# Attention and a gated feed-forward layer: the end of a query softmax moved back in VectorE's queue, four buffers for decode and sums, 64-wide kv, queries in place

## The chip, the cores and the metric

One core of a Trainium2 chip runs the whole program. The metric is the device time of one execution in microseconds; the figure before is the median of three runs. Names: PE is TensorE (PEld its weight loads), DVE is VectorE, ACT is ScalarE, POOL is GpSimd, SP the engine that issues most DMAs.

## The reference

All data are float32. There are 8 sequences of 576 tokens, 8 heads of 64. The attention has no matrix of scores: queries are softmaxed over the 64 numbers of a head, keys over the sequence, and a 64x64 matrix kv per sequence and head stands between them. Its output, 4608 tokens of 512 numbers, goes through a layer of 2048 hidden units.

```python
q_s = exp(q - max(q, axis=-1)); q_s = q_s / (sum(q_s, axis=-1) + 1e-09)
k_s = exp(k - max(k, axis=2));  k_s = k_s / (sum(k_s, axis=2) + 1e-09)
kv  = einsum('bhsd,bhse->bhde', k_s, v)
x   = einsum('bhsd,bhde->bhse', q_s, kv)      # then (4608, 512)
h   = x @ w_in                                 # 512 x 2048
g   = h * clip(h + 3, 0, 6) / 6
out = g @ w_out                                # 2048 x 512
```

## The kernel before

**Numbers.** Weights come as 64-bit patterns. `decode(f)` turns the pattern of hidden chunk f (128 hidden units, f from 0 to 15) into float32 in the tile v (tag v, a ring of three buffers of 4 KB a partition) and `split`s it into a high part (a cast on ACT) and a low part (a subtraction on DVE), so that a product is three matmuls: high by high, high by low, low by high. `decode` costs ACT three instructions (the absolute value into m, the scaling of raw, the cast to w) and DVE five (two on m, two on v, the subtraction to w).

**Stages.** Tokens 0 to 1535 are three blocks j = 0, 1, 2 of 512. For each block and each chunk f, `gemm1` makes ph = x times w_in (12 matmuls), `relu6` makes g (one instruction on ACT, one on DVE), `split_ahead` makes its two parts gp, and `gemm2` adds 12 matmuls to four accumulators po (four PSUM banks for the whole block, one for each 128 tokens). `store` takes po out of PSUM at the block's end, alternately on ACT and DVE, and writes it out. The remaining 3072 tokens are three superblocks of 1024 (`phase1`, `phase2`), which use a scheme of seven products instead of eight; the sums of weight blocks that it needs are made by `sum_weights` during blocks 1 and 2.

**The attention of the next stage runs between the chunks.** Four head pairs hp of two heads each. `attention(j, hp)` serves blocks 0 and 1, `token_attention` the rest. Each is a generator whose pieces are called by `steps` between the chunks: keys (maximum, exponential, transposes pe and pe2, copies to ke), queries (maximum qm, exponentials with their sums qr, division, transposes tp, copy to qT), then `kv_of` (products pkv, rk, kv) and the product px of kv with qT, whose result is split into the next block's x. In `attention` for block 1 the query softmax is eight ACT instructions of 64 columns with the sum taken along; DVE then adds EPS to qr, takes the reciprocal and multiplies.

**kv.** For two heads, kv is a 128x128 tile with the two 64x64 matrices on the diagonal and zeros elsewhere, made by one DVE instruction that multiplies by a mask; px of both heads is then one matmul. A float32 matmul is two instructions in the profile. Only superblocks 1 and 2 have kv for their new sequences as 128x64 tiles (`narrow`), and run px in 64x64 quarters of PE, each head in a PSUM bank of its own.

**The order of the work.** A scheduler orders each engine's instructions by a cost model and by priorities; `ahead` notes the last instruction of g, gp and w on each engine in `front`, and `behind` makes its work issue after those. From block 1 on PE keeps the order in which the program is written (`in_order`); the other engines, and PE in block 0, stand in the order that the scheduler chose. Each engine and SP's queue then run strictly in that order.

**sum_weights.** Each pair of chunks and each side takes two v buffers: w4 (the weights, loaded from DRAM for pairs 3 to 7) and sums (four combinations). Both are split in place and stored by four DMAs (`keep`). Pairs from DRAM take two calls, and one call is made per chunk, from chunk 4 of block 1 on.

Of the kernel before, what the change touches and what calls it, by code (L numbers as in the profile page):

```python
# [19 lines left out]
P = 128  # L20
# [13 lines left out]
def attention_moe(  # L34
# [63 lines left out]
    mask = const.tile([P, P], F32, name="mask")  # L98
    nc.gpsimd.memset(mask, 0.0)
    nc.gpsimd.memset(mask[0:D, 0:D], 1.0)  # L100
    nc.gpsimd.memset(mask[D:P, D:P], 1.0)
# [44 lines left out]
    def decode(f):  # L146

        n = 2 * DM
        pairs = raws.pop(f).rearrange("p (n two) -> p n two", two=2)
        low, high = pairs[:, :, 0], pairs[:, :, 1]  # L150
        m = moe.tile([P, n], F32, name="m", bufs=1)
        nc.scalar.activation(m, high.bitcast(F32), AF.Abs)
        nc.vector.tensor_scalar(m, m, W_MIN, W_MAX, op0=ALU.max, op1=ALU.min)
        m = m.bitcast(U32)
        nc.vector.tensor_scalar(
            m, m, 3, 0x3FFFFFFF, op0=ALU.logical_shift_left, op1=ALU.bitwise_and
        )
        v = moe.tile([P, n], F32, name="v", bufs=3)
        vu = v.bitcast(U32)
        nc.vector.scalar_tensor_tensor(  # L160
            vu, high, 0xC0000000, m, op0=ALU.bitwise_and, op1=ALU.bitwise_or
        )
        nc.scalar.activation(low, low, AF.Copy, scale=2.0**-29)
        nc.vector.tensor_tensor(vu, vu, low, op=ALU.add)
# [19 lines left out]
    narrow = set()  # L184
# [8 lines left out]
    first = {}  # L193

# [12 lines left out]
    def kv_of(hp, batches, quarters=False):  # L207
        n = len(batches)
        both = bank_a("pkv")[:, 0 : n * (D + 1)].rearrange("p (b d) -> p b d", b=n)
        for i, (_, ke, vt) in enumerate(batches):  # L210
            for c in range(NCH):
                for h in range(2):
                    hs = slice(h * D, (h + 1) * D)
                    mm(both[hs, i], ke[:, c, hs], vt[:, c, h, :], c == 0, c == NCH - 1, n > 1)
        rk = att.tile([P, 2], F32, name="rk", bufs=2)[:, 0:n]
        nc.vector.tensor_scalar_add(rk, both[:, :, D], EPS)
        nc.vector.reciprocal(rk, rk)
        for i, (b, _, _) in enumerate(batches):
            kv = att.tile([P, P], F32, name="kv", bufs=10)
            if quarters:  # L220
                nc.vector.tensor_scalar_mul(kv[:, 0:D], both[:, i, 0:D], rk[:, i : i + 1])
                kvs[b, hp] = kv
                narrow.add((b, hp))
                continue
            nc.vector.scalar_tensor_tensor(
                kv.rearrange("p (h d) -> p h d", h=2),
                both[:, i : i + 1, 0:D].broadcast_to([P, 2, D]),
                rk[:, i : i + 1],
                mask.rearrange("p (h d) -> p h d", h=2),
                op0=ALU.mult,  # L230
                op1=ALU.mult,
            )
            kvs[b, hp] = kv
# [6 lines left out]
    def q_softmax(qt, lean, pool):  # L240
# [18 lines left out]
        nc.vector.tensor_scalar_add(qr, qr, EPS)  # L259
# [16 lines left out]
    def attention(j, hp):  # L276
# [3 lines left out]
        else:  # L280
# [9 lines left out]
        q_softmax(qt, j > 0, nc.vector if j else nc.gpsimd)  # L290
# [5 lines left out]
        if j:  # L296
            qT = att.tile([P, TB], F32, name="qT")
# [54 lines left out]

    held = {}
# [7 lines left out]
    def token_attention(t0, n, hp, put):  # L361
# [40 lines left out]
        kv_of(hp, list(zip(new, ke, vt)), t0 >= START + SB)  # L402
# [8 lines left out]
    def sb_attention(s):  # L411
        def put(t0, hp, need, qT):

            if not s:
                for c in range(SB // TB):
                    px = bank_a("px")
                    for b, lo, hi in segments(need, t0 + c * TB):
                        mm(px[:, lo:hi], kvs[b, hp], qT[:, c * TB + lo : c * TB + hi], True, True)
# [4 lines left out]
            for both in zip_longest(*(segments(need, t0 + c * TB) for c in range(2))):  # L423
                for c, part in enumerate(both):
                    if part:
                        b, lo, hi = part
                        for h, r in enumerate(rows):
                            mm(
                                px[h][rows[c], lo:hi],
                                kvs[b, hp][r, slice(0, D) if (b, hp) in narrow else r],  # L430
# [11 lines left out]
    def block_attention(j):  # L442
        def put(t0, hp, need, qT):
            px = bank_a("px")
            for b, lo, hi in segments(need, t0):
                mm(px[:, lo:hi], kvs[b, hp], qT[:, lo:hi], True, True)
# [35 lines left out]
    def sum_weights(pair, side):  # L482

        w4 = moe.tile([P, 2 * DM], F32, name="v", bufs=3)
# [10 lines left out]
        sums = moe.tile([P, 2 * DM], F32, name="v", bufs=3)  # L495
# [86 lines left out]
    def phase1(s):  # L582
        xb, yb, zb = {}, {}, {}
        for i, (p, n) in enumerate(SLOTS1):
# [24 lines left out]
            with tc.high_priority():  # L609
# [14 lines left out]
                if n == 6:  # L624
                    nc.vector.tensor_add(h21, h21, y)
                    r = moe.tile([P, 2 * DM], F32, name="v", bufs=3)
# [3 lines left out]
    def phase2(s):  # L630
# [30 lines left out]
        def outs(name):  # L661
            return moe.tile([P, 2 * DM], F32, name="v", bufs=3).rearrange("p (c n) -> p c n", c=2)
# [107 lines left out]
    def store(j, po):  # L770
        for t in range(NTT):
            if j == NB - 1:
                ob = moe.tile([P, 2 * DM], F32, name="v", bufs=3)[:, 0:DM]
# [67 lines left out]
    for j in range(NB):  # L841
        if j == 1:
            in_order.append(True)
        if j < NB - 1:
# [4 lines left out]
            else:  # L849
                step = steps(units, 3, (2,))  # L850
# [3 lines left out]
        for n, f in enumerate(chunks):  # L854
# [9 lines left out]
            if j > 1 or j and n > 3:  # L864
# [99 lines left out]
```

## Time and profile before

| | |
|---|---|
| runs | 827.92, 828.76, 829.11 us; median 828.76 |
| profiled execution | 827.1 us; span 825.3 us, mean granted clock 0.996 |
| busy | PE 97%, DVE 82%, ACT 55%, POOL 7% of the span |
| PE idle, 0 to 35.83 us | 13.4 us (loads, block 0's own attention, first decodes) |
| PE idle, 35.83 to 140.73 us (block 0) | 4.3 us |
| PE idle, 140.73 to 337.11 us (blocks 1, 2) | 3.8 us |
| PE idle, 337.11 us to the end (superblocks) | 4.9 us |

The span is the time from the first to the last instruction; 1.8 us lie around it. A row of the timeline has the start, the duration, the engine, the line, the operation, the tile written and those read, and in brackets the idle time before it with what ended it. Matmul ends are modelled, and back-to-back matmuls overlap, so their pace is taken from long groups.

### The profile page before, as it was taken

The page shows a single profiled execution, that of the slowest core. Times are in us where ns is not written, and L with a number is a line of the kernel's source. Part 1 is how long each engine was busy: PE and PEld are TensorE (multiplying, and loading weights), DVE is VectorE, ACT ScalarE, POOL GpSimd, SP SyncE. Part 2 cuts the span into 40 slices and gives each one's busy share as a digit, 9 for nine tenths or more (in the row PEclk, how much of TensorE's full clock was granted, in tenths as well). Part 3 has the DMA queues.
Part 4 walks back from the last instruction along what each step waited for, and adds up shares of the span by engine and source line. Part 5 has one row for each costly group of instructions (what it writes and reads, how often), then busy time and mean ns, then how long its engine had stood idle before and what let it go on. Part 6 is the DMA issues. An engine that isn't in the chain of part 4 may idle for free.

```text
span 825.3 us, 11783 instructions
## 1 busy us (share of the span) xinstructions
PE 798.8 (97%) x4088; PEld 641.3 (78%) x4088; DVE 673.4 (82%) x1064; ACT 454.1 (55%) x733; POOL 55.7 (7%) x155
## 2 busy tenths in 40 slices
PE   4899899999989999999999999999999999999998
PEld 3577678888877778887877788777788888888886
DVE  7998998589979888888999994798699836658873
ACT  7897673334444445556556653565556535445543
POOL 5000001010111110001003000011000000000000
PEclk9999999999999999999999999999999999999999
DMA  9999676245579873888786677775566776666673
GB/s 368 416 407 334 199 263 225 59 163 189 192 239 341 288 263 128 267 279 277 272 279 213 187 233 251 226 234 183 178 184 199 238 247 197 187 201 185 197 218 114
DMA packets 75803, 192.30 MB, mean 233 GB/s; under 512 B 7264, under 2 KB 19808, under 8 KB 73696
## 3 DMA queue, kind: packets, MB, share of 16 engines
q1 hardware_dynamic: 75024, 190.38, 70.1%
q10 hardware_dynamic: 720, 1.18, 0.4%
q8 instruction: 32, 0.52, 0.3%
q14 instruction: 27, 0.22, 0.1%
HBM read 147.49 MB, written 44.04 MB: 232 GB/s over the span
## 4 chain that ended last, share of the span: by engine, by line
PE 69%; DVE 16%; DMA 7%; ACT 4%; issue 3%; SPq 1%; POOL 1%; DVEq 0%; ACTq 0%; POOLq 0%
PE x L88 29%; PE z L88 11%; PE y L88 11%; PE ph L88 7%; PE po L88 7%; DMA wf<-v 4%; DMA qt<-in_qf_dram 2%; PE px L88 2%; DVE g L580 1%; PE pkv L88 1%; DVE v L160 1%; DVE qt L343 1%; DVE v L121 1%; DVE gp L121 1%; DVE m L350 1%
## 5 line engine op out<-in xcount | busy, mean ns | idle before, releaser
L121 ACT CAST gf<-g 128x512 fp32r<-128x512 f32 x168 | 104.2, 622 | 97.5 <-DVE gf L121 37.0
L88 PE MATMUL po<-w,gp 128*128 128x512 f32 x576 | 145.5, 399 | 3.6 <-DVE gp L779 2.1
L88 PE MATMUL ph<-x,w 128*128 128x512 f32 x576 | 142.7, 394 | 3.2 <-ACT w L121 2.0
L121 DVE TENSOR_TENSOR gf<-g,gf 128x512 fp32r<-128x512 f32 x168 | 112.9, 686 | 25.3 <-ACT gf L121 24.9
L88 PEld LDWEIGHTS ph<-x,w 128*128 128x128 f32 x576 | 107.8, 188 | 29.6 <-ACT w L121 3.0
L88 PEld LDWEIGHTS po<-w,gp 128*128 128x128 f32 x576 | 106.7, 189 | 29.2 <-DVE gp L779 2.5
L88 PE MATMUL x<-right,gp 128*128 128x512 f32 x384 | 94.6, 391 | 0.4 <-ACT g L616 0.4
L88 PE MATMUL x<-gf,gp 128*128 128x512 f32 x384 | 94.1, 390 | 0.0
L88 PEld LDWEIGHTS x<-gf,gp 128*128 128x128 f32 x384 | 71.9, 188 | 15.7 <-DVE gf L121 0.4
L88 PEld LDWEIGHTS x<-right,gp 128*128 128x128 f32 x384 | 71.6, 188 | 15.7 <-ACT g L616 0.8
L579 ACT ACTIVATE g<-ph,three 128x512 f32<-128x512 f32 x48 | 32.7, 684 | 38.1 <-PE ph L88 38.1
L88 PE MATMUL y<-right,gp 128*128 128x512 f32 x192 | 49.1, 391 | 0.0
L88 PE MATMUL x<-right,left 128*128 128x512 f32 x192 | 47.7, 392 | 0.0
L88 PE MATMUL x<-gf,left 128*128 128x512 f32 x192 | 47.0, 390 | 0.0
L88 PE MATMUL z<-gf,gp 128*128 128x512 f32 x192 | 46.9, 390 | 0.0
L333 POOL COPY swap<-qm 32x32 f32<-32x32 f32 (+1 forms) x64 | 19.6, 306 | 355.3 <-DVE qm L341 353.3
L121 ACT CAST gp<-g 128x512 fp32r<-128x512 f32 x48 | 29.7, 619 | 23.8 <-DVE g L580 23.7
L88 PEld LDWEIGHTS z<-gf,gp 128*128 128x128 f32 x192 | 36.0, 188 | 7.8 <-DVE gf L121 0.4
L88 PEld LDWEIGHTS x<-gf,left 128*128 128x128 f32 x192 | 35.9, 188 | 7.7 <-ACT v L702 0.2
L88 PEld LDWEIGHTS y<-right,gp 128*128 128x128 f32 x192 | 35.8, 188 | 7.6 <-issue 0.2
L88 PEld LDWEIGHTS x<-right,left 128*128 128x128 f32 x192 | 35.7, 188 | 7.6
L580 DVE SCALAR_TENSOR_TENSOR g<-g,ph 128x512 f32<-128x512 f32 x48 | 32.6, 680 | 9.2 <-ACT g L579 9.1
(139 smaller groups left out, 1279.8 us busy)
## 6 DMA issues: line engine op xcount, KB each, us to landing
gp<-wf SPq DMA_DIRECT2D x112, 512.0 KB, 4.2
left<-wf SPq DMA_DIRECT2D x56, 512.0 KB, 4.2
raw<-in_w_dram SPq DMA_DIRECT2D x16, 1024.0 KB, 13.6
wf<-v SPq DMA_DIRECT2D x64, 256.0 KB, 3.2
wf<-w SPq DMA_DIRECT2D x48, 256.0 KB, 4.5
vt<-in_v_dram SPq DMA_DIRECT2D x28, 325.0 KB, 5.6
kt<-in_kT_dram SPq DMA_DIRECT2D x28, 288.0 KB, 3.8
ke<-in_k_dram SPq DMA_DIRECT2D x24, 320.0 KB, 5.1
```

The lines of the kernel that those rows point to most:

```text
L88: nc.tensor.matmul(out, lhsT, rhs, start=start, stop=stop, skip_group_check=goes_on)
L121: return nc.scalar.copy(hi, src), nc.vector.tensor_sub(lo, src, hi.bitcast(F32))
L160: nc.vector.scalar_tensor_tensor(vu, high, 0xC0000000, m, op0=ALU.bitwise_and, op1=ALU.bitwise_or)
L333: nc.gpsimd.tensor_copy(swap[r : r + QD], stat[o : o + QD])
L343: nc.vector.tensor_sub(qs, qs, across(qm))
L350: nc.vector.transpose(qT, qt)
L579: ahead(nc.scalar.activation(r, h, AF.Relu, bias=three, scale=1.0))
L580: ahead(nc.vector.scalar_tensor_tensor(g, r, 6.0, h, op0=ALU.min, op1=ALU.mult))
```

## The change

1. In block 1's attention the query softmax stops after the exponentials (`yield`); the addition of EPS to qr comes a step later and is made to issue after the instructions in `front`, so on DVE behind the last g, gp or w of the next chunk. Each unit has four steps instead of three, and its last piece (px) is called in the second step of the next unit.
2. Queries are softmaxed, transposed and stored back in one tile of two halves, used in turn by the head pairs; the tiles qt and qT of before are gone, so that pair hp+1 can be loaded while pair hp is still in use.
3. kv is always 128x64; the mask is gone; every px is two 64x64 matmuls (`heads`), here with both heads in one PSUM bank.
4. The ring of v has four buffers, and the sums begin one chunk earlier.

```diff
-        v = moe.tile([P, n], F32, name="v", bufs=3)
+        v = moe.tile([P, n], F32, name="v", bufs=4)
...
-            kv = att.tile([P, P], F32, name="kv", bufs=10)
-            if quarters:
-                nc.vector.tensor_scalar_mul(kv[:, 0:D], both[:, i, 0:D], rk[:, i : i + 1])
...
-            nc.vector.scalar_tensor_tensor(
-                kv.rearrange("p (h d) -> p h d", h=2),
-                both[:, i : i + 1, 0:D].broadcast_to([P, 2, D]),
-                rk[:, i : i + 1],
-                mask.rearrange("p (h d) -> p h d", h=2),
...
+            kv = att.tile([P, D], F32, name="kv", bufs=10)
+            nc.vector.tensor_scalar_mul(kv, both[:, i, 0:D], rk[:, i : i + 1])
             kvs[b, hp] = kv
...
-        nc.vector.tensor_scalar_add(qr, qr, EPS)
+        with ExitStack() as order:
+            if lean:
+                yield
+
+                for ins in front.values():
+                    order.enter_context(tc.issue_after(ins.ins))
+            nc.vector.tensor_scalar_add(qr, qr, EPS)
         nc.vector.reciprocal(qr, qr)
...
-            qt = att.tile([P, TB], F32, name="qt", bufs=1)
-            nc.sync.dma_start(qt, q[j, hp])
-            qt = qt.rearrange("p (c h d) -> p c h d", c=NC4, h=2)
+            if "q" not in held:
+                held["q"] = att.tile([P, SB], F32, name="qt", bufs=1)
+            qT = held["q"][:, hp % 2 * TB : (hp % 2 + 1) * TB]
+            nc.sync.dma_start(qT, q[j, hp])
+            qt = cut(qT, 0, NC4, 2, D)
...
-        q_softmax(qt, j > 0, nc.vector if j else nc.gpsimd)
+        yield from q_softmax(qt, j > 0, nc.vector if j else nc.gpsimd)
...
-        if j:
-            qT = att.tile([P, TB], F32, name="qT")
         nc.scalar.copy(qT, tp)
...
-                mm(px[:, lo:hi], kvs[b, hp], qT[:, lo:hi], True, True)
+                heads(px, lo, hi, kvs[b, hp], qT, True)
...
+    def heads(px, lo, hi, kv, qT, start):
+
+        for h in range(2):
+            r = slice(h * D, (h + 1) * D)
+            mm(px[r, lo:hi], kv[r], qT[r, lo:hi], start, True, True)
...
-                step = steps(units, 3, (2,))
+                step = steps(units, 4, (1,))
...
-            if j > 1 or j and n > 3:
+            if j > 1 or j and n > 2:
                 behind(sums)
```

What it does to the order, at three places. First ACT in block 0, around 40 us, before (g_356 is the first chunk's g and gp_359 its high part, m and raw belong to decode, kt and ke to the keys of head pair 0 of block 1, qt and qr to its queries):

```order
L152 ACTIVATE m_467<-raw_4_122 128x1024
L265 ACTIVATE kt_373<-kt_373,km_380 128x576
L121 CAST gp_359<-g_356 128x512
L121 CAST w_3_426<-v_422 128x2x512
L272 COPY ke_375<-pe_429 128x512
L273 COPY ke_375<-pe2_430 64x128
L121 CAST gp_415<-g_412 128x512
L163 ACTIVATE raw_7_397<-raw_7_397 128x1024
L247 ACTIVATE qt_378,qr_384<-qt_378,qm_383 128x64 x8
L579 ACTIVATE g_461<-ph_448,three_84 128x512
```

The same place after:

```order
L148 ACTIVATE m_450<-raw_4_118 128x1024
L574 ACTIVATE g_356<-ph_343,three_80 128x512
L256 ACTIVATE kt_373<-kt_373,km_380 128x576
L574 ACTIVATE g_409<-ph_396,three_80 128x512
L117 CAST w_3_423<-v_419 128x2x512
L232 ACTIVATE qt_378,qr_384<-qt_378,qm_383 128x64 x6
L117 CAST gp_359<-g_356 128x512
L232 ACTIVATE qt_378,qr_384<-qt_378,qm_383 128x64 x2
L117 CAST gp_412<-g_409 128x512
L263 COPY ke_375<-pe_461 128x512
```

The two g and six of the eight exponentials now stand ahead of the cast of the first chunk's g, and so does the cast of w_3.

Second DVE in block 0, where the query softmax of head pair 1 ends, before (qm is the maximum, qr the sums):

```order
L121 TENSOR_TENSOR w_8_761<-v_756,w_8_761 128x2x512
L580 SCALAR_TENSOR_TENSOR g_808<-g_808,ph_795 128x512
L245 TENSOR_REDUCE qm_552<-qt_547 128x8
L121 TENSOR_TENSOR gp_811<-g_808,gp_811 128x512
L259 TENSOR_SCALAR qr_553<-qr_553 128x8
L260 RECIPROCAL qr_553<-qr_553 128x8
L261 TENSOR_TENSOR qt_547<-qt_547,qr_553 128x512
```

After; its maximum (qm_550) stands 28 places further up:

```order
L117 TENSOR_TENSOR w_6_603<-v_598,w_6_603 128x2x512
L250 TENSOR_SCALAR qr_551<-qr_551 128x8
L156 SCALAR_TENSOR_TENSOR v_654<-raw_7_394,m_650 128x1024
L117 TENSOR_TENSOR x1_611<-px_606,x1_611 128x512
L117 TENSOR_TENSOR gp_591<-g_588,gp_591 128x512
L251 RECIPROCAL qr_551<-qr_551 128x8
```

The addition to the sum stood two places behind the maximum and now stands 28 behind it.

Third DVE at the end of block 1, before (v_2091 is a sum, gp_2354 and gp_2359 the evictions of po, g_2292 the g of block 2's first chunk):

```order
L580 SCALAR_TENSOR_TENSOR g_2292<-g_2292,ph_2279 128x512
L497 TENSOR_TENSOR v_2091<-v_2022 128x256
L499 TENSOR_TENSOR v_2091<-v_2022 128x256
L350 STREAM_TRANSPOSE m_2340<-qt_2302 128x1024
L368 TENSOR_REDUCE km_2471<-kt_2461 128x1
L498 TENSOR_TENSOR v_2091<-v_2091,v_2022 128x256
L396 TENSOR_TENSOR ke_2255<-ke_2255,pm_2313 128x640
L396 TENSOR_TENSOR ke_2259<-ke_2259,pm_2313 128x640
L121 TENSOR_TENSOR gp_2295<-g_2292,gp_2295 128x512
L779 TENSOR_SCALAR gp_2354<-po_1365 128x512
```

After (the g is g_2303, the sum v_2309):

```order
L331 TENSOR_TENSOR qm_2346<-qm_2346,swap_2349 128x32
L340 TENSOR_TENSOR qt_2324<-qt_2324,qm_2346 128x1024
L342 TENSOR_REDUCE qr_2347<-qt_2324 128x32
L575 SCALAR_TENSOR_TENSOR g_2303<-g_2303,ph_2290 128x512
L363 TENSOR_REDUCE km_2497<-kt_2487 128x1
L391 TENSOR_TENSOR ke_2266<-ke_2266,pm_2339 128x640
L391 TENSOR_TENSOR ke_2270<-ke_2270,pm_2339 128x640
L331 SCALAR_TENSOR_TENSOR qr_2347<-qr_2347,swap_2358 128x32
L117 TENSOR_TENSOR gp_2306<-g_2303,gp_2306 128x512
L492 TENSOR_TENSOR v_2309<-v_2234 128x256
L494 TENSOR_TENSOR v_2309<-v_2234 128x256
L774 TENSOR_SCALAR gp_2380<-po_1366 128x512
```

The sum moved from directly behind g to directly ahead of the first eviction, and the softmax of the next unit (qt, qr) from ahead of g by a whole unit to just ahead of it.

From block 1 on, PE's order differs only in the px products.

More of the change, by code (lines that the diff above doesn't have):

```diff
@@ L97, in attention_moe @@
     make_identity(nc, ident)
[L98 to L101, printed above, removed]
     three = const.tile([P, 1], F32, name="three")
@@ L183, in attention_moe @@
     kvs = {}
-    narrow = set()
     def cut(t, at, *shape):
@@ L193, in attention_moe @@
     first = {}
+    held = {}
     def load_first(hp):
@@ L205, in load_first_v, with kv_of @@
         nc.sync.dma_start(first[hp][3], v[0, hp])
-    def kv_of(hp, batches, quarters=False):
+    def kv_of(hp, batches):
         n = len(batches)
@@ L218, in kv_of @@
         for i, (b, _, _) in enumerate(batches):
-            kv = att.tile([P, P], F32, name="kv", bufs=10)
-            if quarters:
[L221 to L225, printed above, removed]
-                kv.rearrange("p (h d) -> p h d", h=2),
-                both[:, i : i + 1, 0:D].broadcast_to([P, 2, D]),
-                rk[:, i : i + 1],
-                mask.rearrange("p (h d) -> p h d", h=2),
-                op0=ALU.mult,
-                op1=ALU.mult,
-            )
+            kv = att.tile([P, D], F32, name="kv", bufs=10)
+            nc.vector.tensor_scalar_mul(kv, both[:, i, 0:D], rk[:, i : i + 1])
             kvs[b, hp] = kv
@@ L351, in q_softmax_t @@
         return qT
-    held = {}
     def x_of(s):
@@ L401, in token_attention @@
         yield
-        kv_of(hp, list(zip(new, ke, vt)), t0 >= START + SB)
+        kv_of(hp, list(zip(new, ke, vt)))
         yield
@@ L417, in put @@
                     for b, lo, hi in segments(need, t0 + c * TB):
-                        mm(px[:, lo:hi], kvs[b, hp], qT[:, c * TB + lo : c * TB + hi], True, True)
+                        heads(px, lo, hi, kvs[b, hp], qT[:, c * TB : (c + 1) * TB], True)
                     nc.scalar.copy(x_of(s)[:, hp, c * TB : (c + 1) * TB], px)
@@ L429, in put @@
                                 px[h][rows[c], lo:hi],
-                                kvs[b, hp][r, slice(0, D) if (b, hp) in narrow else r],
+                                kvs[b, hp][r],
                                 qT[r, c * TB + lo : c * TB + hi],
@@ L445, in put @@
             for b, lo, hi in segments(need, t0):
-                mm(px[:, lo:hi], kvs[b, hp], qT[:, lo:hi], True, True)
+                heads(px, lo, hi, kvs[b, hp], qT, True)
             x_hi, x_lo = x_block(j)
@@ L482, in sum_weights @@
     def sum_weights(pair, side):
-        w4 = moe.tile([P, 2 * DM], F32, name="v", bufs=3)
+        w4 = moe.tile([P, 2 * DM], F32, name="v", bufs=4)
         if pair < FROM_DRAM:
@@ L494, in sum_weights @@
         a11, a12, a21, a22 = (q1, q3, q2, q4) if side else (q1, q2, q3, q4)
-        sums = moe.tile([P, 2 * DM], F32, name="v", bufs=3)
+        sums = moe.tile([P, 2 * DM], F32, name="v", bufs=4)
         s1, s3, s2, s4 = (sums[:, n * HT : (n + 1) * HT] for n in range(4))
@@ L625, in phase1 @@
                     nc.vector.tensor_add(h21, h21, y)
-                    r = moe.tile([P, 2 * DM], F32, name="v", bufs=3)
+                    r = moe.tile([P, 2 * DM], F32, name="v", bufs=4)
                     relu6(gb, r, gb)
@@ L661, in outs @@
         def outs(name):
-            return moe.tile([P, 2 * DM], F32, name="v", bufs=3).rearrange("p (c n) -> p c n", c=2)
+            return moe.tile([P, 2 * DM], F32, name="v", bufs=4).rearrange("p (c n) -> p c n", c=2)
         def send(t, r, c):
@@ L772, in store @@
             if j == NB - 1:
-                ob = moe.tile([P, 2 * DM], F32, name="v", bufs=3)[:, 0:DM]
+                ob = moe.tile([P, 2 * DM], F32, name="v", bufs=4)[:, 0:DM]
             else:
```

## Prediction

> **What bounds the kernel now.** I read the page first, then the busy time by stage, then the waits, and last the timeline at each place where TensorE (PE) waits.
>
> ```profile
> span 825.3 us, 11783 instructions
> PE 798.8 (97%) x4088; PEld 641.3 (78%) x4088; DVE 673.4 (82%) x1064; ACT 454.1 (55%) x733; POOL 55.7 (7%) x155
> ```
>
> PE is busy 97% of the span, so what can be won is its idle time and what can be lost is any work added to it. The stretches below are: up to the first full use of w_2, the rest of block 0, block 1, block 2, the superblocks.
>
> ```profile
> core 0: us, PE busy (x) PEld busy (x) DVE busy (x) ACT busy (x) POOL busy (x), PEclk, DMA share, GB/s
> 0.00:35.83 35.83, 22.40 (x150) 16.48 (x151) 30.30 (x54) 28.44 (x41) 12.85 (x25) 0.95 0.97 388
> 35.83:140.73 104.90, 100.61 (x503) 78.17 (x504) 98.74 (x144) 77.22 (x155) 2.43 (x10) 0.98 0.82 292
> 140.73:245.85 105.12, 103.00 (x554) 83.01 (x553) 85.99 (x167) 43.84 (x69) 11.71 (x40) 1.00 0.52 169
> 245.85:337.11 91.26, 89.61 (x492) 72.41 (x493) 79.83 (x140) 42.94 (x66) 9.79 (x32) 1.00 0.74 255
> 337.11:825.28 488.17, 483.23 (x2390) 391.27 (x2390) 378.52 (x562) 261.69 (x405) 18.90 (x48) 1.00 0.70 219
> ```
>
> PE idles 4.3 us in the rest of block 0, 2.1 in block 1, 1.7 in block 2. The superblocks keep their PE order and idle 4.9 of 488 us; the change has nothing to win or lose there. In block 0 VectorE (DVE) is nearly as full as PE (98.7 of 104.9 us). The waits of that stretch:
>
> ```profile
> DVE qr L259 <- ACT qt L247: 2.6, 2, 2.0
> PE ph L88 <- ACT w L121: 2.0, 1, 2.0
> PE ph L88 <- DVE w L121: 1.1, 3, 0.5
> PE tp L94 <- DVE qt L261: 0.9, 2, 0.6
> ```
>
> DVE waits 2.0 us for the exponentials of head pair 1, decode runs late behind it, and PE then waits 2.0 us for w_10. That wait costs more than itself:
>
> ```profile
> 91.14:94.56 3.42, 1.54 (x8) 1.09 (x9) 3.42 (x6) 3.18 (x6) 0.00 (x0) 1.00 0.55 211
> 94.56:97.97 3.41, 3.41 (x9) 2.63 (x9) 3.41 (x5) 2.75 (x15) 0.00 (x0) 0.50 0.69 217
> 97.97:101.38 3.41, 3.41 (x18) 2.76 (x17) 3.31 (x7) 3.20 (x7) 0.00 (x0) 1.00 0.67 254
> ```
>
> After a stretch of 3.4 us in which PE was busy for 1.54, the granted clock is 0.50 for 3.41 us: 9 matmuls, not 18, so 1.7 us lost. Block 0 thus holds 4.3 + 1.7 = 6.0 us that could be won.
>
> **The change, part by part.**
>
> *The end of the softmax behind g, queries in place.* The DVE wait above goes: the sum of head pair 1 now stands far behind its maximum. With two halves in the query ring, pair 1's query loads and is exponentiated while pair 0's is still in use, so 16 exponentials fall into the stretch from 40 to 52 us instead of 8, and the DVE g of chunk 0 stands three instructions later. That hits ScalarE (ACT) where it is full:
>
> ```profile
> 35.45 1.25 ACT L579 ACTIVATE g<-ph,three 128x512 f32<-128x512 f32 x2
> 36.95 1.14 ACT L152 ACTIVATE m<-raw 128x1024 f32<-128x1024 f32 x1 [0.25 <-DVE v L160]
> 37.99 0.76 ACT L265 ACTIVATE kt<-kt,km 128x576 f32<-128x576 f32 x1
> 38.65 0.61 ACT L121 CAST gp<-g 128x512 fp32r<-128x512 f32 x1
> 39.70 1.05 ACT L121 CAST w<-v 128x1024 fp32r<-128x1024 f32 x1 [0.44 <-DVE v L164]
> ...
> 42.97 2.66 ACT qt L247 x16
> ```
>
> Before, the cast of chunk 0's g ends at 38.65 + 0.61 = 39.26. After, it stands behind m (1.04 from start to start), two g (0.62 each), the key's exponential (0.66), the cast of w_3 (0.96) and six of the eight exponentials (6/8 of 2.66 = 2.0; the 16 rows are eight exponentials with their reads). The m still waits for the decode step that ended at 36.95: 36.95 + 5.9 + 0.61 = 43.5, so 4.2 us later. PE's next instruction is the second product of chunk 0, which reads this cast:
>
> ```profile
> 38.81 0.76 PE L94 MATMUL pe<-ident,kt 128*128 128x128 f32 x5 [0.39 <-ACT kt L265]
> 39.33 2.08 PE L88 MATMUL po<-w,gp 128*128 128x512 f32 x8
> ```
>
> PE, whose order here is unchanged, therefore stands still from about 39.6 to 43.5, longer than the pause that halved the clock above, so I add 1.7: 5.9 us. What it would have waited until w_4 (0.6 for tp, the longest of its row of waits, and 0.3 in the row of DVE's w) is then covered, 0.9 less: 5.0 us late. Bounds: 0, if nothing is held up, and 5.9. I take 5.0, since each instruction ahead of the cast is in the built order.
>
> From there PE is about 5 us behind a decode that is itself 3 us late (six of pair 1's exponentials stand ahead of the cast of w_4 too: 2.0 us, and about 1 us of DVE's own waits). That leaves some 2 us of slack or more, so the later waits of block 0 go: 4.3 of idle time, less the 0.9 above and the 0.39 at pe, is 3.0, most of it the 2.0 for w_10; with the clock's 1.7, 4.7 us are won back (between 3.0 and 4.7).
>
> *64-wide kv.* DVE gets a shorter eviction:
>
> ```profile
> L225 DVE SCALAR_TENSOR_TENSOR kv<-pkv,rk,mask 128x128 f32<-128x128 f32 x20 | 6.5, 339 | 0.0
> L221 DVE TENSOR_SCALAR kv<-pkv,rk 128x64 f32<-128x64 f32 x12 | 3.0, 277 | 0.1
> ```
>
> 62 ns each, four of them ahead of w_2: 0.25 us won. On PE each px becomes two 64x64 products on the diagonal quarters. The superblocks already run 64x64 quarters, and show what entering and leaving them costs:
>
> ```profile
> 589.22 2.20 PE L88 MATMUL x<-gf,gp 128*128 128x512 f32 x9
> 591.35 1.09 PE L88 MATMUL px<-m,kv 64*64 64x448 f32 x12
> 592.37 1.65 PE L88 MATMUL y<-right,left 128*128 128x512 f32 x6
> ...
> 159.15 1.76 PE L88 MATMUL ph<-x,w 128*128 128x512 f32 x7
> 160.74 1.03 PE L88 MATMUL px<-m,kv 128*128 128x128 f32 x4
> 161.61 0.27 PE L94 MATMUL pm<-ident,km 128*128 128x128 f32 x1
> 161.64 2.09 PE L88 MATMUL po<-w,gp 128*128 128x512 f32 x8
> ...
> 149.04 2.72 PE po L88 x12
> ```
>
> From the end of x (591.42) to the end of y (594.02) are 2.60 us; six matmuls at 2.72/12 = 0.227 take 1.36, leaving 1.24 for px in quarters. From the end of ph (160.91) to the end of po (163.73) are 2.82; less 1.81 for eight matmuls and 0.11 for pm, 0.90 for a whole px of the same 512 columns. A px in quarters costs 0.34 more. Blocks 1 and 2 of the loop hold eight such groups (four units of block 2, four of the first superblock): 2.7 us, and nothing hides it, since PE is the bound there. In block 0 there are six (pairs 2 and 3 have theirs in two pieces): 2.0 us. The four of block 0's own attention stand in PE's idle start. Bounds: 0, if two quarters cost no switch, and 0.34 each.
>
> That needs the two heads to run side by side. In the px row above the quarters' four streams of 512 columns take together what one whole px takes, and there each bank takes both column halves at once; never two row halves, since each head has its own bank. Now both heads write one bank, in different partitions. By the nearest row I take it as free. The Trainium skill (TensorEngine Tiling, "Gotcha 1: PSUM Pressure") says: "Different row tiles cannot access same PSUM bank simultaneously"; no run here shows it, and by that rule each px would take its columns twice, which is rival B.
>
> *Four buffers of v, sums a chunk earlier.* In blocks 1 and 2, DVE waits with a sum for the stores that still read its buffer, and what stands behind it is the eviction of po:
>
> ```profile
> 236.62 0.68 DVE L580 SCALAR_TENSOR_TENSOR g<-g,ph 128x512 f32<-128x512 f32 x1
> 240.25 0.43 DVE L497 TENSOR_TENSOR v<-v 128x256 f32<-128x256 f32 x1 [2.95 <-DMA wf<-v]
> 245.12 0.68 DVE L779 TENSOR_SCALAR gp<-po 128x512 f32<-128x512 f32 x1
> ...
> 245.85 1.66 PE L88 MATMUL po<-w,gp 128*128 128x512 f32 x6 [2.13 <-DVE gp L779]
> ...
> 282.75 0.43 DVE L497 TENSOR_TENSOR v<-v 128x256 f32<-128x256 f32 x1 [1.89 <-DMA wf<-v]
> ...
> 287.75 1.20 PE L88 MATMUL po<-w,gp 128*128 128x512 f32 x4 [0.84 <-DVE gp L121]
> ...
> 233.24 7.00 DMA wf<-v
> ```
>
> A store takes up to 7.0 us here. With four buffers a sum overwrites what was stored a pair earlier, about two chunks (10.9 us), so both waits go, and with them PE's 2.13 and 0.84: 3.0 us won. Bounds: 0, if another wait takes their place, and 3.8, PE's whole idle time of both blocks. What is late next there is the softmax of the next unit, which now stands half a step further back, with its own exponential to wait for; from g at 236.62 the po eviction would be reached near 243.5, just as PE needs it (its six matmuls from 242.2 end at 243.6).
>
> *The rest* (no mask, the mask's memsets on POOL, a 256 KB query load on SP's queue ahead of the load of raw_14) I cost at nothing: POOL is 7% busy, and w_14 is decoded last but one.
>
> **The sum.** Block 0: +5.0 - 4.7 + 2.0 - 0.25 = +2.1. Blocks 1 and 2: +2.7 - 3.0 = -0.3. Together +1.8 us. The profiled execution took 827.1 us (span 825.3), so 828.9 for it; the median of the runs is 828.76, which gives 830.6. The measurement can tell about 0.2%, 1.7 us, from no change.
>
> **The rivals.**
> A, faster: PE's pause at chunk 0 is short. It decides when pause and half clock together cost under 2.4 us in place of 5.9 (the sum is then below -1.7). If ACT reaches the cast 2 us sooner and the clock stays full, they cost 2.2 and the sum is -1.9, 826.9; with no pause at all it is -3.2, 825.6. For it speaks that the same engines were within 0.4 us of each other here before; against it, that ACT was full (the rows from 36.95 on run nearly without a gap).
> B, much slower: the heads of a px run one after the other, in 16 streams of 512 columns (four each in blocks 1 and 2, eight in the first superblock) at about 0.85: +13.6, 844.
> C, slower: four buffers do not do at the block's end what they should; the eviction of po is held by the softmax that moved next to it. The 3.0 do not come: 833.6.
> D, faster: two diagonal quarters cost no switch: 4.7 less, 825.9.
>
> **Chances and range.** Forecast 830.6 with 828.6 to 832.6 as its own range: 0.48, half of it within 0.2%, half above. A 0.24 (0.18 faster, 0.06 same). B 0.07. C 0.14. D 0.07 (0.05 faster, 0.02 same). So faster 0.23, same 0.32, slower 0.45. A range from 825.5 to 834.0 leaves out B, and of A and C the far ends.
>
> **What would show it.** Around 40 us PE idle for 3 to 4 us before po, released by ACT's cast, and a clock of 0.50 in the 3.4 us after it; no wait of 2 us for w_10 and no half clock near 95; px groups of 64*64 at 1.24 us per 512 columns; no wait of DVE for wf<-v above 1 us, and no wait of po near 245. The prediction is wrong if the pause near 40 is missing or is swallowed by waits for decode that remain, if px takes 2 us, or if PE waits for po at the end of block 1 as before.

## The result, and the profile after

The changed kernel takes 833.12 us (median of 6 runs, 831.23 to 835.79) where the kernel before takes 828.34 (6 runs): a ratio of 1.0061, 95% interval 1.0042 to 1.0079, so 0.6% slower. The forecast was 1.8 us more than before; measured are 4.8. The time lies in the range, 2.5 us above the predicted 830.6, and the terms behind it are not all as forecast; the 1.8 itself lies outside the interval (3.5 to 6.5 us). The profiled execution took 833.6 us, its span is 831.9.

The page of the changed kernel, first lines; then its busy time by stage. The cuts lie at the same points of PE's work as in the table of before, except the one between blocks 1 and 2: here it is the end of block 1's last po, there it lay 6.2 us behind that, in block 2's first po. The two blocks are therefore compared together.

```profile
span 831.9 us, 11908 instructions
PE 803.3 (97%) x4160; PEld 638.7 (77%) x4160; DVE 673.8 (81%) x1064; ACT 453.3 (54%) x733; POOL 58.0 (7%) x152
```

```profile
core 0: us, PE busy (x) PEld busy (x) DVE busy (x) ACT busy (x) POOL busy (x), PEclk, DMA share, GB/s
0.00:37.25 37.25, 22.95 (x158) 16.09 (x158) 30.09 (x54) 28.21 (x40) 12.42 (x22) 0.91 0.97 386
37.25:141.77 104.52, 100.18 (x519) 77.94 (x520) 96.42 (x142) 77.19 (x155) 2.70 (x10) 0.98 0.82 288
141.77:247.19 105.42, 102.31 (x561) 79.49 (x561) 90.11 (x177) 44.70 (x71) 14.43 (x40) 0.98 0.60 195
247.19:342.40 95.21, 93.79 (x534) 74.22 (x533) 78.72 (x133) 41.40 (x64) 9.59 (x32) 1.00 0.64 222
342.40:831.85 489.45, 484.08 (x2390) 390.98 (x2390) 378.49 (x562) 261.81 (x405) 18.90 (x48) 1.00 0.66 217
```

Start to start, the stages are now 1.4 us longer (37.25 against 35.83), 0.4 shorter (block 0), and together 4.25 longer for blocks 1 and 2 (200.63 against 196.38); the superblocks are 1.3 longer. So block 0, where the forecast saw the loss, came out even, and the loss is where it saw a balance. What PE waits for in blocks 0 to 2, by what ended each wait (total, times, longest):

```profile
PE pm L94 <- ACT x L414: 3.4, 2, 2.4
PE po L88 <- ACT gp L117: 3.3, 1, 3.3
PE pe L94 <- ACT kt L256: 1.0, 1, 1.0
PE px L88 <- DVE kv L217: 0.6, 1, 0.6
PE ph L88 <- DVE w L117: 0.5, 1, 0.5
```

The 2.0 for w_10 and the waits of po for DVE's evictions have gone. In their place stand the pause at chunk 0 (po for the cast of its g), as forecast, and a wait that the forecast does not have: pm, in a PSUM bank that px held, for the copies of x out of that px. The place at the end of block 1:

```profile
235.68 1.22 DVE L338 TENSOR_REDUCE qm<-qt 128x32 f32<-128x1024 f32 x1 [2.10 <-DMA qt<-in_qf_dram]
239.00 1.22 DVE L340 TENSOR_TENSOR qt<-qt,qm 128x1024 f32<-128x1024 f32 x1
240.25 1.06 ACT L341 ACTIVATE qt<-qt 128x1024 f32<-128x1024 f32 x1 [6.09 <-DVE qt L340]
241.79 1.06 ACT L414 COPY x<-px 128x512 f32<-128x512 f32 x2
242.42 0.43 PE L94 MATMUL pm<-ident,km 128*128 128x128 f32 x2 [2.38 <-ACT x L414]
```

Read from below: PE has px done at 240.04 and stands 2.38 us for two copies of x. ACT had nothing to do for 6.09 us, but its next instruction was the exponential of the following unit's queries, which needed DVE's subtraction, which needed the maximum, which had waited 2.10 us for the load of the queries. In the kernel before, this maximum was taken some 7 us sooner against PE's work (3.0 us of the 10.2 are the lag that PE has by then):

```profile
225.50 1.22 DVE L341 TENSOR_REDUCE qm<-qt 128x32 f32<-128x1024 f32 x1 [0.41 <-DMA qt<-in_qf_dram]
```

### The profile page after: what moved, and what is told of

It reads as the page before. It is cut to its first block, busy times and chain, and to the rows that moved or that the text cites. A ratio compares the mean times of both kernels' runs of the same rounds, so it can differ in the third digit from the quotient of the medians.

```text
span 831.9 us, 11908 instructions
## 1 busy us (share of the span) xinstructions
PE 803.3 (97%) x4160; PEld 638.7 (77%) x4160; DVE 673.8 (81%) x1064; ACT 453.3 (54%) x733; POOL 58.0 (7%) x152
## 4 chain that ended last, share of the span: by engine, by line
PE 50%; DVE 12%; DMA 7%; ACT 2%; issue 2%; POOL 1%; SPq 0%; DVEq 0%; POOLq 0%
PE x L88 27%; PE z L88 11%; PE y L88 9%; DMA qt<-in_qf_dram 4%; POOL swap L330 1%; DVE g L575 1%; DVE m L347 1%; PE po L88 1%; DVE qt L340 1%; DMA wf<-v 1%; DVE qm L338 1%; DVE qt L345 1%; DVE qr L342 1%; DMA v<-whole 1%; PE px L88 1%
## 5 line engine op out<-in xcount | busy, mean ns | idle before, releaser
L88 PE MATMUL y<-right,gp 128*128 128x512 f32 x192 | 49.1, 391 | 0.0
L330 POOL COPY swap<-qm 32x32 f32<-32x32 f32 (+1 forms) x64 | 22.2, 347 | 359.0 <-DVE qm L338 341.7
L574 ACT ACTIVATE g<-g,three 128x512 f32<-128x512 f32 x24 | 17.4, 725 | 39.0 <-DVE g L608 38.9
```

The costliest lines, as they stand in the source:

```text
L88: nc.tensor.matmul(out, lhsT, rhs, start=start, stop=stop, skip_group_check=goes_on)
L330: nc.gpsimd.tensor_copy(swap[r : r + QD], stat[o : o + QD])
L574: ahead(nc.scalar.activation(r, h, AF.Relu, bias=three, scale=1.0))
```

## The experiments

Twelve kernels, each timed against the kernel before on its own chip. For each, the length of the stages in its profile: to the end of block 0, block 1, block 2 (each to the end of its last matmul on po), and the rest.

| kernel | ratio to before (95%) | to end of block 0 | block 1 | block 2 | rest |
|---|---|---|---|---|---|
| before | 1 | 140.7 | 98.9 | 100.1 | 485.6 |
| changed | 1.0061 (1.0042-1.0079) | 141.8 | 105.4 | 97.8 | 486.9 |
| 1 64-wide kv alone | 1.0191 (1.0167-1.0216) | 144.5 | 100.2 | 105.9 | 487.7 |
| 2 softmax end and queries | 1.0030 (1.0012-1.0049) | 141.5 | 98.9 | 99.0 | 486.3 |
| 3 changed, three buffers | 1.0181 (1.0145-1.0218) | 143.9 | 100.2 | 110.3 | 486.6 |
| 4 changed, 128-wide kv | 1.0021 (1.0009-1.0034) | 139.3 | 102.6 | 99.7 | 486.3 |
| 5 changed, x first | 1.0091 (1.0073-1.0109) | 140.5 | 100.3 | 100.8 | 490.2 |
| 6 changed, first cast ahead | 1.0140 (1.0119-1.0161) | 150.7 | 103.1 | 97.9 | 485.7 |
| 7 number 4, x first | 1.0033 (1.0017-1.0050) | 140.0 | 100.5 | 100.7 | 489.8 |
| 8 number 3, query queue | 1.0171 (1.0139-1.0203) | 145.0 | 100.2 | 98.8 | 493.8 |
| 9 changed, no softmax end | 1.0088 (1.0063-1.0112) | 142.6 | 103.5 | 97.8 | 488.0 |
| 10 softmax end alone | 1.0040 (1.0024-1.0056) | 144.9 | 98.9 | 99.3 | 487.3 |
| 11 number 4, sums later | 0.9996 (0.9982-1.0011) | 138.9 | 98.9 | 99.1 | 490.1 |
| 12 number 4, query queue | 1.0088 (1.0066-1.0110) | 140.5 | 105.5 | 100.6 | 486.8 |

A stage of one profile is uncertain by 1.7 us or a multiple, since a stretch of half clock may or may not fall into it (last section).

**1. 64-wide kv alone.** The kernel before with part 3:

```diff
-            kv = att.tile([P, P], F32, name="kv", bufs=10)
+            kv = att.tile([P, D], F32, name="kv", bufs=10)
+            nc.vector.tensor_scalar_mul(kv, both[:, i, 0:D], rk[:, i : i + 1])
...
-                mm(px[:, lo:hi], kvs[b, hp], qT[:, lo:hi], True, True)
+                heads(px, lo, hi, kvs[b, hp], qT, True)
```

> The kernel before with part 3 alone: kv 64 wide, every px in two 64x64 quarters; three buffers, separate query tiles, the softmax in one piece. In the built order the six exponentials already stand ahead of the cast of chunk 0's g here, so the place of that cast comes from the shorter kv in the scheduler's plan and not, as the prediction had it, from the two halves of the query ring. Quarter theory (a switch costs 0.34 us for each 512 columns): 12 px are 4.1 us, kv 0.25 less, and the pause at chunk 0 with its half clock as in the changed kernel (3.3 us and about 1.5), of which other waits win back some 4: 828.3 + 4.1 - 0.25 + 1 = 833, with PE released by ACT's cast near 43 us. Rival (quarters cost nothing, the loss of the changed kernel is all waits of block 1): 829, px groups at 0.9 us for 512 columns.

842.9 against 827.2, far above both. The pause at chunk 0 is there, by the same 3.25 us:

```profile
42.34 0.62 ACT L117 CAST gp<-g 128x512 fp32r<-128x512 f32 x1
43.01 1.22 PE L88 MATMUL po<-w,gp 128*128 128x512 f32 x2 [3.25 <-ACT gp L117]
```

So the 64-wide kv (its eviction and the quarters together) brings the pause, with neither the queries in place nor the moved softmax end. How it leads the scheduler to this order is not shown. The largest part of the loss was expected by nobody: block 2 is 5.8 us longer, by one wait of po for gp of 3.7 us near 321 with a half clock behind it. Number 3 has it too, and number 8 looks for its cause.

**2. The softmax end and the queries in place, without parts 3 and 4** (the mask and the whole px are back as well).

```diff
-            kv = att.tile([P, D], F32, name="kv", bufs=10)
+            kv = att.tile([P, P], F32, name="kv", bufs=10)
-        v = moe.tile([P, n], F32, name="v", bufs=4)
+        v = moe.tile([P, n], F32, name="v", bufs=3)
```

> The changed kernel with parts 3 and 4 undone: the softmax end is behind the next g and queries are in place, but kv is 128 wide with its mask, px one matmul for both heads, three buffers, sums as before. Theory (the pause is not owed to the queries): no pause near 40 us, since the cast stands where it stood; DVE's wait of 2.0 us for the exponentials, PE's 2.0 for w_10 and the half clock of 1.7 behind it are gone: 828.3 - 3.5 = 825, between 824 and 827; blocks 1 and 2 as before, PE waiting 2.1 and 0.8 for po. Rival (the prediction's wording: the second half of the query ring brings the exponentials forward and with them the pause): 828.5, a pause of 3 us near 40.

829.7 against 827.2. There is no pause: the first cast stands where it stood, and PE goes on from pe to po.

```profile
38.55 0.60 ACT L121 CAST gp<-g 128x512 fp32r<-128x512 f32 x1
38.70 0.77 PE L94 MATMUL pe<-ident,kt 128*128 128x128 f32 x5
39.22 2.09 PE L88 MATMUL po<-w,gp 128*128 128x512 f32 x8
```

With number 1, that settles whose the pause is. The hoped 3.5 us did not come: PE waits elsewhere in block 0 instead (1.2 for the transposed queries at 49.1, 1.8 for w_10 again at 94.1). DVE's wait of 2.0 us for the exponentials at qr is gone, but at 84.1 DVE waits 1.2 us for the ACT part of g, which stands behind eight exponentials on ACT, and w_10 comes as late as before.

**3. The changed kernel with three buffers of v,** sums from chunk 4 (bufs=3 and n > 3, as before the change).

> The changed kernel with part 4 alone undone: three buffers of v, sums from the fourth chunk as before. Ring theory (with four buffers two sums at a time go ahead on DVE, the next unit's softmax slips by about a chunk, its exponential stands ahead of the copies of x on ACT, and PE waits 2.4 + 1.0 us at pm, 0.6 for kv, 1.5 for the half clock): these 5.5 go, and PE's waits of 2.1 and 0.8 for po with some 0.5 of small ones come back: 833.1 - 2 = 831. Rival (the softmax end one step later is what makes the units late): pm still waits for x and the po waits come back as well: 836.

842.9 against 827.2, above both and 1.2% more than with four. So beside the quarters the fourth buffer, with the sums a chunk earlier, is worth about 10 us, where the theory had it cost 2. Both are true in part: block 1 is 5.2 us shorter with three buffers, and there is no wait for x; block 2 is 12.5 longer.

**4. The changed kernel with 128-wide kv** (the mask back, px whole, a ring of nine kv for room; four buffers).

> The changed kernel with part 3 alone undone: kv 128 wide with its mask (ring of nine kv instead of ten, for room), px one matmul, four buffers. Ring theory: the kernel with three buffers and wide kv plus some 2 us of net loss in blocks 1 and 2 (pm released by ACT's x, about 2.4 us at the end of block 1): 827. Quarter theory: px takes 0.9 us for 512 columns again, so against the changed kernel 14 x 0.34 = 4.7 us come back and the pause of block 0 with them: 833.1 - 4.7 - 1 = 827 as well; the two differ in the trace, by the wait at pm. Rival (four buffers pay 3 us once the px is short, since kv and x are then in time): 822, no wait at pm near 240.

829.0 against 827.2. Taking back part 3 alone wins back about 3 of the 5 us (1.8 over the kernel before in place of 4.8). The wait at pm is there without the change's quarters (0.1 at 238.7, 0.4 at 259.2, 2.1 at 281.3), and block 1 has 102.6 us against 98.9 in number 2, which differs by the buffers and sums (and by nine kv for ten): the ring theory's half of the answer. Of the waits at pm only the first lies in block 1; PE's other waits there are 0.7 for kv and 0.8 and 1.0 for gp.

**5. The changed kernel with x first.** The exponential is made to issue after the copies of x of the unit before:

```diff
-        nc.scalar.activation(qt, qt, AF.Exp)
+        with ExitStack() as order:
+            if last_x:
+                order.enter_context(tc.issue_after(last_x.pop().ins))
+            nc.scalar.activation(qt, qt, AF.Exp)
```

> The changed kernel, and in blocks 1 and 2 the exponential of the next unit's queries is made to issue after the copies of x of the unit before, on ACT. Order theory (the exponential that waits for its late softmax stands ahead of the copies of x, and PE waits for them): the waits at pm of 2.4 and 1.0 us and the half clock of 1.7 go, 5 us in all, and nothing takes their place: level with the kernel before, 828.5 where that takes 828.3. Rival (the slip of the softmax on DVE is what costs, and it holds up the next g or the eviction of po as well): the waits move to po, 831 to 833.

834.8 against 827.9: no gain. Block 1 did fall by the 5.1 us that the order theory gave (105.4 to 100.3, no wait at pm), so the cause of that wait is shown. But block 2 took 3.0 of them back, in four waits of po for gp (1.1 at 311.3 the longest), and the rest of the run took 3.3. PE comes to the first superblock 3.3 us sooner, and there waits for a factor with a half clock behind it. On DVE that factor (the right at 345.86) stands behind a subtraction for another one and an eviction of po:

```profile
344.12 1.22 DVE L573 TENSOR_TENSOR x<-x 128x1024 f32<-128x1024 f32 x1
345.25 0.69 DVE L778 TENSOR_SCALAR v<-po 128x512 f32<-128x512 f32 x1
345.86 1.22 DVE L117 TENSOR_TENSOR right<-x,right 128x1024 fp32r<-128x1024 f32 x1
347.13 2.21 PE L88 MATMUL x<-right,left 128*128 128x512 f32 x5 [2.50 <-DVE right L117]
```

The x of the last unit is not what it waits for: ACT had copied it by 301.4.

**6. The first cast ahead.** In block 0 the exponentials, and the scaling in the decode of chunks 2 to 4, issue behind the cast of chunk 0's g:

```diff
+                if lead:
+                    order.enter_context(tc.issue_after(lead[0].ins))
                 for i in range(n8):
                     nc.scalar.activation(
```

> The changed kernel, and in block 0 the exponentials (of the keys and the queries of block 1) and the scaling in the decode of chunks 2 to 4 issue on ACT behind the cast of chunk 0's g. The pause of 3.3 us before the first po and its half clock go. Step of the prediction (the pause is won back by the waits that its slack covers, 4.7 us): the others return, DVE and PE wait for decode near 50 and 93 as in the kernel before, and the time stays within 1 us of the changed kernel's 833. Rival (block 0 has room, the pause is a plain loss): 5.2 us less, 828.

839.2 against 827.9: a miss for both. The edit moved the pause instead of taking it away: the decode that was pushed back is late, and PE waits 3.4 us at 42.8 for the keys and 5.3 at 49.5 for w. It says only that ACT is full around 40 us and that something must be late there; whether a pause without such a price would be a plain loss is not tested by it.

**7. Number 4 with x first.**

> Four buffers, queries in place, the softmax end behind the next g, but kv 128 wide with its mask (ring of nine), and the exponential behind the copies of x as in the run above. By the order theory the kernel without that last edit (829.0 where the kernel before takes 827.2) loses its waits at pm (2.1, 0.4 and 0.1) and one half clock (1.7): 824.7, 0.3% under the kernel before. Rival (as above): waits for po in their place, 828 to 829.

829.7 against 827.9, as number 4 within its interval: the 824.7 did not come. As in number 5, the waits at pm go, and 2.5 us of wait for a factor come at 346.6, and px now waits for the transposed queries (0.8 at 235.4, 1.8 at 277.7).

**8. Number 3 with the query loads on another queue** (those of block 2 and the superblocks):

```diff
-        nc.sync.dma_start(
+        nc.gpsimd.dma_start(
             qt.rearrange("p (b n) -> p b n", n=TB),
```

> The changed kernel with three buffers (842.9), and the loads of the queries of block 2 and the superblocks issued from POOL's queue in place of SP's. Queue theory (with three buffers a query load stands on SP's queue behind the load of a weight pair that waits for a v buffer: transposition at 311, load issued at 316.5, maximum at 321.7, and g behind it on DVE): the wait of PE of 4.4 us near 325 goes with its half clock of 1.7, and part of the 3.9 us near 250: 835 or less. Rival (the load is late because it is slow): 842, the same wait near 325.

In number 3, before the wait of block 2 (issues on SP's queue, the maximum, and po):

```profile
310.87 1.24 DVE L347 STREAM_TRANSPOSE m<-qt 128x1024 f32<-128x1024 f32 x1
...
316.02 0.37 SPq L486 DMA_DIRECT2D v<-whole  x1
316.49 0.43 SPq L379 DMA_DIRECT2D qt<-in_qf_dram  x1
...
321.72 1.22 DVE L338 TENSOR_REDUCE qm<-qt 128x32 f32<-128x1024 f32 x1 [4.01 <-DMA qt<-in_qf_dram]
323.46 0.68 DVE L575 SCALAR_TENSOR_TENSOR g<-g,ph 128x512 f32<-128x512 f32 x1
...
324.84 4.60 PE L88 MATMUL po<-w,gp 128*128 128x512 f32 x12 [4.43 <-ACT gp L117]
```

The query tile is free at 312.1, but its load stands behind a weight load that waits until 316.0 for a v buffer; the maximum waits for the load, g stands behind the maximum, and PE waits 4.4 us for gp. From POOL's queue, in number 8:

```profile
308.92 0.73 POOL L379 DMA_DIRECT2D qt<-in_qf_dram  x1 [6.16 <-ACT x L414]
...
312.75 1.22 DVE L338 TENSOR_REDUCE qm<-qt 128x32 f32<-128x1024 f32 x1 [0.60 <-DMA qt<-in_qf_dram]
```

Block 2 falls from 110.3 to 98.8 us: the queue theory holds there. The run as a whole (841.7 against 827.9, the rival's number without the rival's wait) gains little, since the superblocks, whose loads moved too, are 7.2 us longer (PE waits 2.9 us at 431.4 for a g of ACT).

**9. The changed kernel without part 1** (the softmax of block 1 in one piece, three steps).

> The changed kernel with part 1 alone undone: the query softmax of block 1 in one piece, three steps to a unit; 64-wide kv, queries in place, four buffers. In the built order the six exponentials still stand ahead of chunk 0's cast and the exponential ahead of the copies of x at the end of block 1. Theory (part 1 only takes DVE's waits for the exponentials in block 0, and PE was not waiting for these): block 0 within 2 us of the changed kernel's 102.0 us, blocks 1 and 2 the same, 832 to 835 where the kernel before takes 828. Rival (part 1 is what keeps block 0 short with the pause in it): block 0 near 106 as in the kernel with 64-wide kv alone, 837.

835.1 against 828.0. Its interval overlaps with the changed kernel's, so part 1 is worth 0.3% or nothing; the rival's 106 us for block 0 did not come (to its end 142.6 us against 141.8).

**10. Part 1 alone** on the kernel before (`yield` and the order behind g, four steps).

> The kernel before with part 1 alone: the softmax end behind the next g, four steps to a unit; kv 128 wide, separate query tiles, three buffers. Theory (as above, part 1 is worth little): block 0 within 1 us of 102.3, blocks 1 and 2 as before, 828 where the kernel before takes 828, within 0.2%. Rival (the wait for w_10 goes with its half clock and nothing comes in its place): 824 to 825.

831.4 against 828.0: slower by 0.4%, a miss for both. Part 1 alone does not even remove DVE's wait: at 81.27 DVE waits 2.8 us for the exponentials, where it was 2.0. PE's wait for w_10 shrinks to 0.4 us, but it waits 1.6 us for gp at 81.7 and 1.9 for w at 111.4, with two stretches of half clock behind the latter.

**11. Number 4 with the sums from chunk 4.**

```diff
-            if j > 1 or j and n > 2:
+            if j > 1 or j and n > 3:
```

> Four buffers, 128-wide kv (ring of nine), queries in place and the softmax end behind the next g, as in the run that took 0.21% more than the kernel before, but the sums begin at chunk 4 of block 1 as they did before the change. Crowding theory (with four buffers the sums of block 1 go two at a time ahead of the softmax on DVE, and the softmax of the next unit comes late): one call less in block 1, the exponential no longer ahead of the copies of x in the built order; block 1 falls from 102.6 to about 100 and the half clock of block 2 goes: 825 where the kernel before takes 827.5, 0.3% under it. Rival (the sums are only pushed later and meet the factors of the first superblock): 829, with a wait for a factor near 345 as in the run with x first.

828.1 against 828.0, a ratio of 0.9996: no difference from the kernel before. The hoped 825 did not come, but each theory was right about a part. Block 1 is back at 98.9 us, so the 3.7 us that number 4 has more there come from starting the sums a chunk earlier. The softmax is not less crowded for it: nine sums fall into block 1 here as in number 4, and the next unit's maximum comes later still (at 239.07, where number 4 has it at 231.10). In the order built, its exponential (242.88) now stands behind the copies of x (233.98 and 234.85), as number 5 forced it to. To the end of block 0 it takes 138.9 us, the shortest of all. The rest is 490.1 us, with 1.9 us of wait for a factor at 341.8 and a half clock.

**12. Number 4 with the query loads of block 2 and the first superblock on POOL's queue.**

> Four buffers, 128-wide kv (ring of nine), queries in place, the softmax end behind the next g, sums from chunk 3 (the kernel that took 0.21% more than before), and the query loads of block 2 and of the first superblock on POOL's queue; the later ones stay on SP's. Queue theory (a query load stands on SP's queue behind weight loads that wait for a v buffer): the softmax comes some 2 to 4 us sooner in blocks 1 and 2, the waits at pm (2.1, 0.4) and the half clock of block 2 go, block 1 falls from 102.6 to about 100: 824.5 where the kernel before takes 828, 0.4% under it. Rival (with four buffers it is the sums on DVE that crowd the softmax, not the load): block 1 stays at 102.6, 829.

835.3 against 827.6: the queue theory fails with four buffers. The load is issued no sooner, and the maximum starts 6.1 us behind its issue where it was 4.1: number 12, then number 4.

```profile
228.90 0.73 POOL L395 DMA_DIRECT2D qt<-in_qf_dram  x1 [8.38 <-issue]
234.99 1.22 DVE L354 TENSOR_REDUCE qm<-qt 128x32 f32<-128x1024 f32 x1 [2.67 <-DMA qt<-in_qf_dram]
```

```profile
227.01 0.38 SPq L395 DMA_DIRECT2D qt<-in_qf_dram  x1
231.10 1.22 DVE L354 TENSOR_REDUCE qm<-qt 128x32 f32<-128x1024 f32 x1 [1.16 <-DMA qt<-in_qf_dram]
```

With four buffers the weight loads in front find a free buffer: during blocks 1 and 2 they wait 3.1 us for stores in number 4, and 30.5 in the kernel before. So nothing was to be won, and POOL's four large loads there took a median of 6.0 us to land, against 5.1 for five of that stretch from SP's queue. PE's waits at pm grow to 3.1, 1.0 and 2.1 us. No version here beats the kernel before.

## Why the prediction was right or wrong, step by step

**The pause at chunk 0: the size was right, its cause wrong.** The cast ended at 44.77, which less the 1.42 us that PE's work is later from the start is 43.35, against 43.5 forecast; PE stood still 0.98 us at pe and 3.25 before po, and the clock was halved from 45.5 to 48.9. The exponentials stand ahead of the cast because of the 64-wide kv (numbers 1 and 2), not of the second half of the query ring. The order was read from the built kernel with all four parts in it, and a reason was put to it that only a kernel with one part could have shown.

**Won back, 4.7: too little.** From 45 us to the end of block 0 PE waits 0.1 us, and each wait of before (w_4, tp, w_9, the 2.0 for w_10 and its half clock) has gone. That the slack of the pause alone does this is not shown: number 1 has the same pause and still waits 1.8 us for w at 103.5. Nor did w_10 hang on DVE's wait for the exponentials, as the prediction read it: in number 2 that wait is gone and PE waits 1.8 us for w_10, in number 10 it is 2.8 us and PE waits 0.4.

The term also missed that a wait costs more than its gap. In the kernel before, twelve matmuls without a wait take 2.72 us from start to start (239.49 to 242.21); the next twelve, with a wait of 2.13 in them, take 5.14:

```profile
239.49 2.88 PE L88 MATMUL ph<-x,w 128*128 128x512 f32 x12
242.21 1.52 PE L88 MATMUL po<-w,gp 128*128 128x512 f32 x6
245.85 1.66 PE L88 MATMUL po<-w,gp 128*128 128x512 f32 x6 [2.13 <-DVE gp L779]
247.35 2.88 PE L88 MATMUL ph<-x,w 128*128 128x512 f32 x12
```

That is 0.29 us beyond the gap; the other waits of ph and po in these two traces give 0.27 to 0.29. Some ten waits shrank to four, about 1.7 us; with PE's attention work there at +1.2 (13.95 against 12.75, each group counted to the end of the first matmul behind it, less that one's 0.227 and the waits) in place of +2.0 it accounts for nearly all of block 0's -0.4 in place of +2.1.

**px in quarters: right.** A px of one block-2 unit, from the end of ph to the end of po:

```profile
159.73 2.20 PE L88 MATMUL ph<-x,w 128*128 128x512 f32 x9
161.87 1.08 PE L88 MATMUL px<-m,kv 64*64 64x128 f32 x8
162.88 0.32 PE L94 MATMUL pm<-ident,km 128*128 128x128 f32 x1
162.96 3.00 PE L88 MATMUL po<-w,gp 128*128 128x512 f32 x12
```

161.93 to 165.96 are 4.03 us; less 12 x 0.227 = 2.72 and 0.11 for pm, 1.20 against the forecast 1.24. Over the eight groups of blocks 1 and 2 the px groups with their pm cost 2.35 us more (14.64 against 12.29, counted in the same way), forecast 2.7. Rivals B and D fall: two heads in one bank run side by side, their matmuls starting 0.01 us apart. The Trainium skill (TensorEngine Tiling, "Gotcha 1: PSUM Pressure") says that different row tiles cannot access the same PSUM bank at one time; here two row halves that write different partitions of one bank take 1.20 us, where one after the other they would take an estimated 2.1 (twice the 0.90 of a whole px and 0.3 for the switch).

**The ring's 3.0: the step that failed.** DVE's waits for wf<-v went as forecast at the end of block 1, and so did PE's 2.13 and 0.84 for po. In their place came 2.38 and 1.00 at pm, 0.61 for kv, and a half clock of 1.7. The working asked what is late next, named the softmax of the next unit, and followed it only along DVE to the eviction of po ("near 243.5, just as PE needs it"). It did not follow it to ACT, where the copies of x are queued behind its exponential. Rival C had the right kind of end (the gain missing because of that softmax) at the wrong place. The step also took the fourth buffer for something that only removes waits. It let more sums into block 1 (38 of their additions on DVE in place of 28; to the end of its last po DVE is busy 90.1 us, 80.4 before), and the softmax, whose tile is loaded only after the transposition before, slipped. The slip goes with part 4: in the six kernels with three of them, the maximum shown above (235.68) starts 11.1 to 13.3 us ahead of the end of the px of the unit before, in the five with four buffers and early sums 3.2 to 7.4. What makes PE wait at pm is ACT's order: in numbers 5, 7 and 11 the maximum comes 3.6 to 4.3 us behind that px, the copies of x stand ahead of the exponential, and PE does not wait at pm. And its worth depends on the rest: 10 us with the quarters (number 3 against the changed kernel), within the measurement's reach nothing with whole px (number 2 against 4).

**Not in the sum.** The start is 1.4 us longer, by a second stretch of half clock near 21 us (PEclk 0.91 against 0.95). Numbers 1 and 5 have the same edit there and a start like that of before (the first 36 matmuls on ph are done at 38.6 us; 38.4 before, 39.8 here), so this is not the change; the six runs of the changed kernel had mean clocks of 0.990 to 0.996 with 835.8 to 831.2 us. The superblocks' 1.3 us are not explained: in kernels with the same PE order there the rest varies from 485.6 to 493.8 us, by small waits for g and factors.

By terms: block 0 came out 2.5 us better than its term, blocks 1 and 2 4.5 worse, and 2.7 came from where nothing was forecast. That the total lies near the predicted time is partly this cancelling, and so luck; so is that rival C's 833.6 lies nearer still, since the eviction of po, which was to be late by it, was not.

## What to carry to other kernels

When a wait is taken away, follow what is late next on every engine that has something queued behind it: an instruction that waits in order holds whatever stands behind it, here copies of x whose px was done. A deeper ring also lets its users run ahead, and on an engine that is 82% busy they do so in front of someone else; price it together with the queues (SP's among them) that its users share. Where a reordering is read from a built kernel with several edits, build each edit alone before naming its cause.

## What the runs showed of the hardware

**The half clock comes in windows that lie on a fixed grid.** The points where it sets in lie whole multiples of 3.413 us apart within a run: 19.46 and 94.56 before (22.0 windows), 18.18, 45.49 and 243.46 after (8.0 and 58.0 windows). What counts is PE's work in such a window, not the length of a wait. The changed kernel, in the window that holds the wait at pm and the next one:

```profile
240.05:243.46 3.41, 1.04 (x6) 0.92 (x7) 2.29 (x4) 2.87 (x5) 0.64 (x4) 1.00 0.27 102
243.46:246.87 3.41, 3.41 (x10) 2.64 (x9) 3.41 (x8) 2.36 (x5) 0.17 (x1) 0.50 0.53 121
```

Number 9 has the same wait of 2.38 us at the same place (242.87), but an edge of its grid, at 241.15, falls into it:

```profile
237.73:241.15 3.42, 2.59 (x19) 1.02 (x17) 2.70 (x6) 0.44 (x1) 1.33 (x4) 1.00 0.99 375
241.15:244.56 3.41, 1.69 (x9) 1.43 (x10) 2.77 (x4) 3.07 (x6) 0.82 (x4) 1.00 0.06 22
244.56:247.97 3.41, 3.41 (x17) 2.83 (x16) 3.41 (x8) 2.05 (x4) 0.00 (x0) 1.00 0.75 207
```

No half clock follows. From some 15 us on, where the traces begin to record the clock, windows at full clock in which PE was busy for up to 1.55 us were followed by one; between that and 1.8 us the busy time alone does not decide (1.69 here was not, 1.78 in number 8 was). So the same wait costs 2.4 or 4.1 us by where the grid lies, and times of one kernel can differ by steps of 1.7 us. The Trainium skill (TensorE: Matmul & The Clock Gate, "Part 1: The HAM clock gate") states a free-running window of 3413 ns, and these points agree; its advice in the section "Why this matters for your kernels", no idle gaps above about 3 us, is too mild for these runs, where 2.0 us (w_10 before) were enough.

**A wait costs PE about 0.28 us beyond its gap,** as worked out above.
